# A spectral mixing and gated MLP kernel on one core: first item's copies, first loads, fewer warming matmuls, two loads on another queue

## The chip, the cores and the metric

The kernel runs on one core of one Trainium2 chip. The metric is the device time of one execution in microseconds (us). All times below are us unless marked ns. The profile comes from one profiled execution. Engines are called as the profile calls them: PE is TensorE (matmuls), PEld its weight loads, DVE is VectorE, ACT is ScalarE, POOL is GpSimd, SP is SyncE, which only issues DMAs here. A "q" behind an engine means its sequencer, which issues DMAs.

## What is computed

With x of 2048 x 512 (A_x; B_x isn't used), in float32:

```python
g = sigmoid((x * gate_w).sum(-1, keepdims=True))
a = dft_seq_re @ (x @ dft_hid_re.T) - dft_seq_im @ (x @ dft_hid_im.T)
b = (silu(x @ w1) * (x @ w3)) @ w2          # w1, w3: 512 x 1376, w2: 1376 x 512
out = g * a + (1 - g) * b
```

## The kernel before, in words

**Precision.** TensorE reads float32r operands. Every float32 operand is split in two: a high part, which is the source copied by ScalarE to float32r (`high`, L108), and a low part, which is source minus high part, subtracted by VectorE (`low`, L111). A product is then three matmuls, high x high, high x low, low x high (`mm3`, `matmul`, L122), accumulated in a PSUM bank of 128 x 512.

**Fast products.** Matrices are cut into 2 x 2 blocks and multiplied with seven block products instead of eight. This is why sums of blocks are formed on VectorE: `SUMS` for x (T1 to T4, L216), `sums_wb` for the weights (L255 to L258), `sum_c` (L698, L701) for the sequence matrices.

**First stage, the items.** An item is one chunk of 128 columns of w1 and w3 (the last chunk also holds the gate vector) with one half of the 2048 positions. `ITEMS` lists 9 chunks with half 0, then 2 chunks with both halves, then 9 with half 1. `gate_up(n)` does item n: groups of six matmuls, in order X (wb), Z (wb), the first product of item n+3 (X, wa), X (wb), Z (wa), the second product of item n+3 (Y, wa), X (wb). Between these, ScalarE and VectorE copy banks, form silu(gate) x up (L399, L414, in tile h), and split the weights of the items ahead. `store_h` sends the two halves of h to DRAM (hsp) from POOL's queue (L339). The lists `early`, `ahead`, `second`, `mid`, `at_end` hold further work for a given item. After each `prod(x, n, 3, 3)` VectorE adds the bank to u4 (L390), and `prod(x, n, 6, 2)` writes that bank again.

**Item 0** is written out by hand, with eight products instead of seven, since its operands arrive one after another. Loads all stand on SP's queue: the first weight block (128 KB, L233), the x block B11 (512 KB, L209), the other three weight blocks, then x blocks B21, B12, B22 and the weights of items 1 to 3. While they arrive, 11 matmuls of a constant run on TensorE (WARM, L425). Its four PSUM banks C00, C01, C10, C11 hold the two gate halves and the two up halves. Silu of C00 and C01 is made on ScalarE (tiles s1 and g1, L484, L500), and VectorE multiplies them with C10 and C11 straight from PSUM (L490, L508). `half(0, 0, 0, 0, ...)` is the first group; its order is high x high and low x high on the first half of B11, the same on the second half, then the two with B11's low part. `half(1, 0, None, 0, ...)` is the second group, on the fourth weight block (tile a). The next groups (wa, 12 matmuls) use B21.

**Second stage, the steps (P).** 12 matmuls a step for the first blocks, from about 207 on. Operands (zo) are split three steps ahead (`split_c(m + 3)`), summed four ahead, loaded eight ahead from SP's queue (B, L724). Functions in `todo` run ahead of a step's matmuls: `gates(0)` ahead of step 2 is ScalarE's sigmoid of the scores (tile p5g, L782), for which `load_score(0)` reads the scores from DRAM (gs), spread over all partitions; it stands right after the last item, on SP's queue (L772). `load_score(1)`, a block later, is on POOL's queue. Behind `gates(0)` in ScalarE's order stands `split_c(5)`. `late_load(i)` (L803) reads later weights, five or six steps ahead of their sums.

**Order.** The program order is kept as written on each engine and queue; an engine's instruction that waits holds up all behind it on that engine.

Of the kernel before, what the change touches and what calls it, by code (L numbers as in the profile page):

```python
# [7 lines left out]
F32 = mybir.dt.float32  # L8
F32R = mybir.dt.float32r
AF = mybir.ActivationFunctionType  # L10
ALU = mybir.AluOpType

P = 128
# [8 lines left out]
NG = NST // 2  # L22
NC = (F + P - 1) // P
NP2 = (NC + 1) // 2
WARM = 11
LOOK = 3
K = 9
W2_AT = (9, 11, 13, 15)
# [4 lines left out]
def fnet_swiglu_gate_kernel(  # L33
# [20 lines left out]
    nc = tc.nc  # L54

    def pool(name, bufs, side, space=None):
        kw = {} if space is None else {"space": space}
        cm = tc.tile_pool(name=name, bufs=bufs, side=side, reuse_waits="tile", **kw)
        return cm, cm.__enter__()
# [9 lines left out]
    xo0_cm, xo0 = pool("xo0", 1, "left")  # L69
    f4_a_cm, f4_a = pool("f4_a", 1, "right")  # L70
    wu_cm, wup = pool("wu", 1, "right")
    s1_cm, s1p = pool("s1", LOOK + 1, "right")
    wa_cm, wap = pool("wa", LOOK + 1, "right")
    wb_cm, wbp = pool("wb", 2, "right")
    u4_cm, u4p = pool("u4", 1, "right")
    h_cm, hp = pool("h", 2, "right")
    xo1_cm, xo1 = pool("xo1", 1, "right")
    gate_pools = (wu_cm, s1_cm, wa_cm, wb_cm, u4_cm, h_cm, xo1_cm)

    def bank(k, name):  # L80
        return psum.tile([P, 512], F32, tag=f"ps{k}", name=name)
# [14 lines left out]
    def wide(name):  # L96
        return take(F4, [P, 1024], F32, name)
# [9 lines left out]
    def high(hi, src):  # L107
        nc.scalar.activation(hi, src, AF.Copy)  # L108

    def low(hi, lo, src):  # L110
        nc.vector.tensor_sub(lo, src, hi.bitcast(F32))  # L111

    def split(hi, lo, src):
        high(hi, src)
        low(hi, lo, src)
# [5 lines left out]
    def matmul(ps, u, v, some=slice(None), **kw):  # L121
        nc.tensor.matmul(ps.rearrange("p (n a) -> p n a", a=2), u, turns(v)[:, some], **kw)  # L122

    def mm3(ps, ah, al, bh, bl, first, last, chain=False, some=slice(None)):
        for n, (u, v) in enumerate(((ah, bh), (ah, bl), (al, bh))):
            matmul(ps, u, v, some, start=first and n == 0, stop=last and n == 2,
                   skip_group_check=chain)
# [13 lines left out]
    def flat(ap):  # L141
        return ap.rearrange("p a n -> p (a n)")
# [33 lines left out]
    def forms2(r, t2, some):  # L176
# [4 lines left out]
        if 1 in some:  # L181
# [7 lines left out]
    ITEMS = ([(c, 0) for c in range(K)] + [(c, g) for c in range(K, NC) for g in range(2)]  # L189
             + [(c, 1) for c in range(K)])  # L190
    NI = len(ITEMS)
    SETS, WSET = [], []
# [5 lines left out]
    XO, ST = {}, {}  # L198
    XRAW = ("B12", "B11", "B21", "B22")

    def flat_x(ap):
        return ap.rearrange("p q n -> p (q n)")

    def load_xo(g, k):

        if g not in XO:
            XO[g] = (xo1 if g else xo0).tile([P, 2, 7, 2, 512], F32R, tag="xo", name=f"xo{g}")
        ST[g, k] = wide(f"xs{g}_{k}")
        nc.sync.dma_start(ST[g, k], xt[g, XRAW.index(k)])  # L209

    OPS = ("B11", "B21", "B22", "T1", "T2", "T3", "T4")
    SUMS = {"T1": ("B12", "B11"), "T2": ("B22", "T1"), "T3": ("B22", "B12"), "T4": ("B21", "T2")}

    def sum_xo(g, k, t):
        ST[g, k] = t
        nc.vector.tensor_sub(t, *(ST[g, v] for v in SUMS[k]))  # L216

    def xo_parts(g, k):
        o = XO[g][:, :, OPS.index(k)]
        return flat_x(o[:, 0]), flat_x(o[:, 1]), ST[g, k]  # L220

    def split_xo(g, k):
        split(*xo_parts(g, k))

    WS, WA, WB = {}, {}, {}
# [1 line left out]
    def back(w):  # L227
        return w >= NC and SETS[w] > 0

    def load_w(w, lo=0, hi=4):  # L230
        if lo == 0:
            WS[w] = f4_a.tile([P, 4, 256], F32, tag=f"f4_{4 + w % (LOOK + 1)}", name=f"ws{w}")
        nc.sync.dma_start(WS[w][:, lo:hi].rearrange("p a n -> p (a n)"),  # L233
                          w13[SETS[w], :, lo * 256 : hi * 256])

    def load_wb(w, spare=False):

# [4 lines left out]
    def wa_parts(w, lo, hi):  # L242
        return (*(flat(WA[w][:, h, lo:hi]) for h in range(2)), flat(WS[w][:, lo:hi]))

    def new_wa(w):

        WA[w] = wap.tile([P, 2, 3, 256], F32R, tag="wa", name=f"wa{w}")
# [27 lines left out]
    def prod(ps, n, wi, xi, start, chain=False):  # L275
        w = WSET[n]
        w, wi = (WA[w], wi) if wi < 3 else (WB[w], wi - 3)
        x = XO[ITEMS[n][1]]
        for q in range(2):
            sl = slice(q * P, (q + 1) * P)  # L280
            mm3(ps, w[:, 0, wi, sl], w[:, 1, wi, sl], x[:, 0, xi, q, :], x[:, 1, xi, q, :],
                start and q == 0, q == 1, chain)

    G = {}
# [4 lines left out]
    def prod1(n):  # L289
        x = bank(n % 4, f"X{n}")  # L290
        prod(x, n, 0, 0, True)
        return x
# [20 lines left out]
    def gate1(n):  # L313
        nc.scalar.activation(G[n][1], G[n][1], AF.Silu)
# [19 lines left out]
    def store_h(n, k, h):  # L334

        c, g = ITEMS[n]
        j = min(c % (NP2 - 1) if c < NC - 1 else NP2 - 1, NP2 - 1)
        b = 2 * (NP2 - 1 <= c < NC - 1)
        nc.gpsimd.dma_start(hsp[g, b + k, j // 2, :, j % 2 * 512 : (j % 2 + 1) * 512], h)  # L339
# [4 lines left out]
    early, ahead, second, mid, at_end = {}, {}, {}, {}, {}  # L344
# [72 lines left out]


    ctx.enter_context(tc.manual_schedule())
    load_w(0, 0, 1)  # L420
    load_xo(0, "B11")
    warm = nc.const_aps.tensor(1.0, [P, 512], mybir.dt.bfloat16)
    wps = bank(7, "wps")
    for n in range(WARM):
        nc.tensor.matmul(wps, warm[:, :P], warm, start=True, stop=True)  # L425
    nc.scalar.activation(act0, warm[:, :24], AF.Silu)
    load_w(0, 1, 4)
    for k in ("B21", "B12", "B22"):
        load_xo(0, k)
    load_w(1)  # L430
# [6 lines left out]
    C = {(i, j): bank((0, 4, 6, 7)[2 * i + j], f"C{i}{j}") for i in range(2) for j in range(2)}  # L437

    def half(i, j, w, x, start):

        wp = lambda h, sl: a21[:, h, sl] if w is None else WA[0][:, h, w, sl]
        xp = lambda q, h: b12[:, h, q * 512 : (q + 1) * 512] if x is None else XO[0][:, h, x, q, :]
        hh, lh, hl = (0, 0), (1, 0), (0, 1)
        order = [(r, *p) for r in range(2) for p in ((hh, hl, lh) if w is None else (hh, lh, hl))]
        if w == x == 0:
            order = [(r, *p) for some in ((hh, lh), (hl,)) for r in range(2) for p in some]
        for n, (r, u, v) in enumerate(order):
            matmul(C[i, j], wp(u, slice(r * P, (r + 1) * P)), xp(r, v),  # L450
                   start=start and n == 0, stop=not start and n == 5)

    def xo_half(k, q):
        i = OPS.index(k)
        return XO[0][:, 0, i, q], XO[0][:, 1, i, q], ST[0, k][:, q * 512 : (q + 1) * 512]

    s1 = s1p.tile([P, 512], F32, tag="s1", name="s1_0")
    g1 = u4p.tile([P, 512], F32, tag="u4", name="g1_0")
    h0 = hp.tile([P, 1024], F32, tag="h", name="h0")
    t1 = hp.tile([P, 1024], F32, tag="h", name="t1")  # L460
    new_wa(0)
    split(*wa_parts(0, 0, 1))

    def split_by_both(hi, lo, src):

        high(hi[:, :256], src[:, :256])
        nc.vector.tensor_copy(hi[:, 256:], src[:, 256:])
        low(hi, lo, src)

    split_by_both(*xo_half("B11", 0))  # L470
    split(*xo_half("B11", 1))
    half(0, 0, 0, 0, True)
    split(a21[:, 0], a21[:, 1], WS[0][:, 3])
# [7 lines left out]
    split(b12[:, 0], b12[:, 1], ST[0, "B12"])  # L481
    half(1, 0, 2, 1, False)
    split_xo(0, "B22")
    nc.scalar.activation(s1, C[0, 0], AF.Silu)  # L484
    half(0, 1, 0, None, True)
    WS.pop(0)
    load_w(4)
    sum_xo(0, "T1", t1)
    half(1, 1, None, None, True)
    nc.vector.tensor_mul(h0[:, :512], s1, C[1, 0])  # L490
    store_h(0, 0, h0[:, :512])
    sum_xo(0, "T2", ST[0, "B11"])
    half(0, 1, 1, 2, False)
    for w in (1, 2):
        new_wa(w)
        split(*wa_parts(w, 0, 3))
    half(1, 1, 2, 2, False)
    free(*zt)
    split_xo(0, "T2")
    nc.scalar.activation(g1, C[0, 1], AF.Silu)  # L500
    x1 = prod1(1)
    sums_wb(1)
    high(*xo_parts(0, "T1")[::2])
# [1 line left out]
    high(*wa_parts(3, 0, 3)[::2])  # L505
    y1 = prod2(1)
    copy_x(1, x1)
    nc.vector.tensor_mul(h0[:, 512:], g1, C[1, 1])  # L508
    store_h(0, 1, h0[:, 512:])
    x2 = prod1(2)  # L510
    high_wb(1)
    sum_g(1, y1)
# [2 lines left out]
    copy_x(2, x2)  # L515
    sum_xo(0, "T3", ST[0, "B12"])
    gate1(1)
    x3 = prod1(3)
    low_wb(1)
    high(*xo_parts(0, "T3")[::2])  # L520
# [7 lines left out]
    def do(work, n, f, *a):  # L528
        work.setdefault(n, []).append(lambda: f(*a))
# [9 lines left out]
    do(second, 1, free, *(ST[0, b] for b in ("B11", "B21", "B12", "B22")))  # L539
    do(second, 1, sum_g, 2, y2)  # L540
    do(mid, 1, gate1, 2)
    do(early, 2, sum_g, 3, y3)
    do(mid, 2, gate1, 3)

# [63 lines left out]
    for n in range(NI):  # L608
        if n in W2_AT:
            p = W2_AT.index(n)  # L610
# [4 lines left out]
        if n in A1_AT:  # L615
            p = A1_AT.index(n)
# [9 lines left out]
    n = NI - 1 - LOOK  # L626
# [142 lines left out]
    def load_score(g, queue):  # L769
        t, ng = GATES[g] = [flat(ut.tile([P, 2, 512], F32, tag=k, name=f"{k}g{g}"))  # L770
                            for k in ("p5", "u2")]
        queue.dma_start(t.rearrange("p (b n) -> p b n", b=2),  # L772
                        gs[2 * g : 2 * g + 2].rearrange("b o n -> o b n").to_broadcast([P, 2, 512]))
# [1 line left out]
    high_a(NG - 1)  # L775
    low_a(NG - 1)
    advance(-1)
    load_score(0, nc.sync)

    def gates(g):  # L780

# [18 lines left out]
    def late_load(i, src, tag):  # L800

        r, m = (flat(ut.tile([P, 2, 512], F32, tag=k, name=f"{k}p{i}")) for k in (tag, "c21"))
        nc.sync.dma_start(r, src)  # L803
        LATE[i] = [r, m]

    def late_pair(i, j):
# [207 lines left out]
    for i, (src, sp, p) in enumerate(late):  # L1014
        blk, b = 1 + i // 3, i % 3
        n = (10, 17, 24)[b]
# [89 lines left out]
```

## Time and profile before

| | |
|---|---|
| runs | 676.85, 676.11, 676.80 (median 676.8) |
| profiled execution | 676.03 |
| its span | 674.3 |
| VectorE busy | 601.5 (89%) |
| ScalarE busy | 370.4 (55%) |
| DMA, mean over the span | 256 GB/s |

The span is what the profile covers; the profiled execution's own time lies 1.7 above it. Busy shares are means over all stages. Matmuls are pipelined, so the duration of one (379 ns) is longer than the distance to the next. A timeline row reads: start, length, engine, line, operation, output <- inputs, shapes, count; in brackets the idle time of the engine ahead of it and what ended that. A windows row reads: stretch, its length, then busy time and count of PE, PEld, DVE, ACT, POOL, the granted clock, DMA share and GB/s. A chain row reads: start, length, what, count.

### The profile page before, as it was taken

Reading aid. Unit: us, or ns where it says so; the run is one execution under the profiler, and the core shown is the slowest. Engines: PE = TensorE matmul, PEld = TensorE weight load, DVE = VectorE, ACT = ScalarE, POOL = GpSimd, SP = SyncE. Lnnn points to the kernel's source line nnn. Section 1 sums busy time; section 2 is a strip of 40 time slices with the busy share of each in tenths; the row PEclk is TensorE's granted clock in tenths of the full one; section 3 lists DMA queues with packets and bytes.
Section 4 is the critical chain, followed back from the end, with each engine's and each line's share of the span. In section 5 each row is a group of like instructions: output and inputs, shape, how many; then the busy total and the mean of one; then the engine's idle time right before and its main releaser. Section 6 shows DMA issues by size and latency. Waiting matters only on the chain.

```text
span 674.3 us, 8670 instructions
## 1 busy us (share of the span) xinstructions
PE 670.3 (99%) x3101; PEld 583.8 (87%) x3101; DVE 601.5 (89%) x748; ACT 370.4 (55%) x494; POOL 64.5 (10%) x119
## 2 busy tenths in 40 slices
PE   9999999999999999999999999999999999999998
PEld 6888888888888888888888888888888888888887
DVE  6999988887679999988999899978896897898996
ACT  6676556655447764465554654554445455445451
POOL 0021112221110000001110101100000000000000
PEclk9999999999999999999999999999999999999999
DMA  7585547599998666815696279918986772873932
GB/s 296 209 306 220 228 192 265 189 337 381 414 418 301 251 215 225 294 63 207 220 387 246 89 246 354 366 57 351 391 330 249 281 256 89 312 279 154 342 130 93
DMA packets 45563, 172.54 MB, mean 256 GB/s; under 512 B 5328, under 2 KB 5712, under 8 KB 41680
## 3 DMA queue, kind: packets, MB, share of 16 engines
q1 hardware_dynamic: 32480, 118.11, 47.8%
q0 software_dynamic: 12752, 53.49, 20.2%
q8 instruction: 24, 0.39, 0.2%
q10 hardware_dynamic: 288, 0.39, 0.2%
q14 instruction: 19, 0.16, 0.1%
HBM read 114.82 MB, written 57.16 MB: 255 GB/s over the span
## 4 chain that ended last, share of the span: by engine, by line
PE 99%; DMA 0%; DVE 0%; ACT 0%; issue 0%
PE P L122 68%; PE X L122 16%; PE Z L122 8%; PE Y L122 4%; PE C L122 2%; PE wps L425 1%; DMA out<-zc 0%; DVE zc L856 0%; ACT zc L863 0%
## 5 line engine op out<-in xcount | busy, mean ns | idle before, releaser
L122 PE MATMUL P<-zo,a 128*128 128x512 f32 x1344 | 290.4, 379 | 0.0
L122 PEld LDWEIGHTS P<-zo,a 128*128 128x128 f32 x1344 | 253.8, 189 | 36.4 <-DVE zo L111 0.4
L108 ACT ACTIVATE zo<-B 128x1024 fp32r<-128x1024 f32 (+1 forms) x182 | 188.4, 1041 | 176.1 <-DVE B L698 74.1
L111 DVE TENSOR_TENSOR zo<-B,zo 128x1024 fp32r<-128x1024 f32 (+1 forms) x182 | 217.4, 1202 | 29.4 <-ACT zo L108 28.8
L122 PE MATMUL P<-zo,H 128*128 128x512 f32 x468 | 101.2, 379 | 0.0
L122 PEld LDWEIGHTS P<-zo,H 128*128 128x128 f32 x468 | 88.5, 189 | 12.6
L698 DVE TENSOR_TENSOR B<-B,B 128x1024 f32<-128x1024 f32 (+1 forms) x78 | 92.8, 1190 | 0.1
L122 PE MATMUL X<-xo,wb 128*128 128x512 f32 x378 | 88.6, 379 | 0.0
L122 PEld LDWEIGHTS X<-xo,wb 128*128 128x128 f32 x378 | 71.4, 189 | 10.2
L122 PE MATMUL P<-zo,Y 128*128 128x512 f32 (+1 forms) x336 | 71.6, 375 | 0.0
L122 PEld LDWEIGHTS P<-zo,Y 128*128 128x128 f32 x336 | 62.7, 189 | 8.7
L339 POOL DMA_DIRECT2D hsp<-h x42 | 23.0, 548 | 121.5 <-DVE h L399 70.4
L701 DVE TENSOR_TENSOR B<-B,B 128x1024 f32<-128x1024 f32 x26 | 31.7, 1219 | 0.0
L122 PE MATMUL X<-xo,wa 128*128 128x512 f32 x126 | 30.8, 380 | 0.0
L122 PE MATMUL Y<-xo,wa 128*128 128x512 f32 x126 | 30.6, 379 | 0.0
L122 PE MATMUL Z<-xo,wb 128*128 128x512 f32 x126 | 30.6, 379 | 0.0
L122 PE MATMUL Z<-xo,wa 128*128 128x512 f32 x126 | 30.6, 379 | 0.0
L122 PEld LDWEIGHTS X<-xo,wa 128*128 128x128 f32 x126 | 23.7, 189 | 3.6 <-DVE wa L111 0.3
L122 PEld LDWEIGHTS Y<-xo,wa 128*128 128x128 f32 x126 | 23.8, 189 | 3.4
L122 PEld LDWEIGHTS Z<-xo,wb 128*128 128x128 f32 x126 | 23.8, 189 | 3.4
L122 PEld LDWEIGHTS Z<-xo,wa 128*128 128x128 f32 x126 | 23.8, 189 | 3.4
L954 ACT ACTIVATE zu<-P 128x512 f32<-128x512 f32 x30 | 17.7, 596 | 15.2 <-PE P L122 12.7
(145 smaller groups left out, 551.4 us busy)
## 6 DMA issues: line engine op xcount, KB each, us to landing
B<-cc SPq DMA_DIRECT2D x64, 512.0 KB, 5.9
hsp<-h POOLq DMA_DIRECT2D x42, 256.0 KB, 3.9
B<-hsp SPq DMA_DIRECT2D x20, 512.0 KB, 5.6
wbsp<-wb POOLq DMA_DIRECT2D x8, 1024.0 KB, 4.2
wb<-wbsp SPq DMA_DIRECT2D x8, 1024.0 KB, 8.0
B<-zsp SPq DMA_DIRECT2D x16, 512.0 KB, 8.4
H<-w2sp SPq DMA_DIRECT2D x6, 1024.0 KB, 9.5
ws<-w SPq DMA_DIRECT2D x11, 512.0 KB, 4.3
```

The lines of the kernel that those rows point to most:

```text
L108: nc.scalar.activation(hi, src, AF.Copy)
L111: nc.vector.tensor_sub(lo, src, hi.bitcast(F32))
L122: nc.tensor.matmul(ps.rearrange("p (n a) -> p n a", a=2), u, turns(v)[:, some], **kw)
L339: nc.gpsimd.dma_start(hsp[g, b + k, j // 2, :, j % 2 * 512 : (j % 2 + 1) * 512], h)
L425: nc.tensor.matmul(wps, warm[:, :P], warm, start=True, stop=True)
L698: nc.vector.tensor_add(t, t, RAW[blk, b, q][:, :n])
L701: nc.vector.tensor_sub(t, RAW[blk, "B12", q], t)
L954: nc.scalar.activation(U[name][:, r], ps[r], AF.Copy)
```

## The change

Five things are done:

- `WARM` is 8 instead of 11.
- The first weight block and the fourth are loaded from ScalarE's queue, ahead of its first activation; the second and third from SP's queue. B11 is loaded in two DMAs of 512 columns. The high part of B11's first half is made by VectorE in one piece, ahead of the low part of the first weight block; before, ScalarE and VectorE made half of it each.
- Of item 0, C10 and C11 are copied from PSUM by ScalarE into a spare tile, beside the two silus. The two multiplications and their stores come later (`finish_first`), at the end of items 3 and 4, from SBUF.
- The spare tile lies where the seventh operand of the second x half will be, which gets a tile of its own (`xo_at`).
- `load_score(0)` and `late_load(0)` are issued from POOL's queue instead of SP's.

```diff
-WARM = 11
+WARM = 8
...
+    def xo_at(g, i):
+        if g == 0 or i < 6:
+            return XO[g][:, :, i]
+        if 2 not in XO:
+            XO[2] = xo1.tile([P, 2, 2, 512], F32R, tag="xo6", name="xo1_6")
+        return XO[2]
...
-        nc.sync.dma_start(ST[g, k], xt[g, XRAW.index(k)])
+        n = 512 if g == 0 and k == "B11" else 1024
+        for b in range(0, 1024, n):
+            nc.sync.dma_start(ST[g, k][:, b : b + n], xt[g, XRAW.index(k), :, b : b + n])
...
-    load_w(0, 0, 1)
+    load_w(0, 0, 1, nc.scalar)
     load_xo(0, "B11")
+    load_w(0, 3, 4, nc.scalar)
...
-    load_w(0, 1, 4)
+    load_w(0, 1, 3)
...
+    spare = xo1.tile([P, 2, 2, 512], F32, tag="xo6", name="spare")
+    first_h = [(spare[:, j, 0], spare[:, j, 1]) for j in range(2)]
+
+    def finish_first(j):
+        s, u = first_h[j]
+        nc.vector.tensor_mul(s, s, u)
+        store_h(0, j, s)
...
-    split(*wa_parts(0, 0, 1))
+    high(*wa_parts(0, 0, 1)[::2])
+    nc.vector.tensor_copy(*xo_half("B11", 0)[::2])
+    low(*wa_parts(0, 0, 1))
+    low(*xo_half("B11", 0))
...
-    split_by_both(*xo_half("B11", 0))
     split(*xo_half("B11", 1))
...
-    nc.scalar.activation(s1, C[0, 0], AF.Silu)
+    nc.scalar.activation(first_h[0][0], C[0, 0], AF.Silu)
...
-    nc.vector.tensor_mul(h0[:, :512], s1, C[1, 0])
-    store_h(0, 0, h0[:, :512])
...
+    nc.scalar.activation(first_h[0][1], C[1, 0], AF.Copy)
...
-    nc.scalar.activation(g1, C[0, 1], AF.Silu)
+    nc.scalar.activation(first_h[1][0], C[0, 1], AF.Silu)
...
-    nc.vector.tensor_mul(h0[:, 512:], g1, C[1, 1])
-    store_h(0, 1, h0[:, 512:])
...
     gate1(1)
+    nc.scalar.activation(first_h[1][1], C[1, 1], AF.Copy)
...
+    for j in range(2):
+        do(at_end, 3 + j, finish_first, j)
...
-    load_score(0, nc.sync)
+    load_score(0, nc.gpsimd)
...
-        nc.sync.dma_start(r, src)
+        (nc.sync if i else nc.gpsimd).dma_start(r, src)
```

More of the change, by code (lines that the diff above doesn't have):

```diff
@@ L202, in flat_x @@
         return ap.rearrange("p q n -> p (q n)")
+    def xo_at(g, i):
[4 more added lines that the diff above has]
+        return XO[2]
     def load_xo(g, k):
         if g not in XO:
-            XO[g] = (xo1 if g else xo0).tile([P, 2, 7, 2, 512], F32R, tag="xo", name=f"xo{g}")
+            XO[g] = (xo1 if g else xo0).tile([P, 2, 7 - g, 2, 512], F32R, tag="xo", name=f"xo{g}")
         ST[g, k] = wide(f"xs{g}_{k}")
-        nc.sync.dma_start(ST[g, k], xt[g, XRAW.index(k)])
+        n = 512 if g == 0 and k == "B11" else 1024
+        for b in range(0, 1024, n):
+            nc.sync.dma_start(ST[g, k][:, b : b + n], xt[g, XRAW.index(k), :, b : b + n])
     OPS = ("B11", "B21", "B22", "T1", "T2", "T3", "T4")
@@ L218, in xo_parts @@
     def xo_parts(g, k):
-        o = XO[g][:, :, OPS.index(k)]
+        o = xo_at(g, OPS.index(k))
         return flat_x(o[:, 0]), flat_x(o[:, 1]), ST[g, k]
@@ L228, in back, with load_w @@
         return w >= NC and SETS[w] > 0
-    def load_w(w, lo=0, hi=4):
+    def load_w(w, lo=0, hi=4, queue=nc.sync):
         if lo == 0:
             WS[w] = f4_a.tile([P, 4, 256], F32, tag=f"f4_{4 + w % (LOOK + 1)}", name=f"ws{w}")
-        nc.sync.dma_start(WS[w][:, lo:hi].rearrange("p a n -> p (a n)"),
-                          w13[SETS[w], :, lo * 256 : hi * 256])
+        queue.dma_start(WS[w][:, lo:hi].rearrange("p a n -> p (a n)"),
+                        w13[SETS[w], :, lo * 256 : hi * 256])
     def load_wb(w, spare=False):
@@ L277, in prod @@
         w, wi = (WA[w], wi) if wi < 3 else (WB[w], wi - 3)
-        x = XO[ITEMS[n][1]]
+        x = xo_at(ITEMS[n][1], xi)
         for q in range(2):
             sl = slice(q * P, (q + 1) * P)
-            mm3(ps, w[:, 0, wi, sl], w[:, 1, wi, sl], x[:, 0, xi, q, :], x[:, 1, xi, q, :],
+            mm3(ps, w[:, 0, wi, sl], w[:, 1, wi, sl], x[:, 0, q, :], x[:, 1, q, :],
                 start and q == 0, q == 1, chain)
@@ L455, in xo_half @@
         return XO[0][:, 0, i, q], XO[0][:, 1, i, q], ST[0, k][:, q * 512 : (q + 1) * 512]
-    s1 = s1p.tile([P, 512], F32, tag="s1", name="s1_0")
-    g1 = u4p.tile([P, 512], F32, tag="u4", name="g1_0")
-    h0 = hp.tile([P, 1024], F32, tag="h", name="h0")
+    spare = xo1.tile([P, 2, 2, 512], F32, tag="xo6", name="spare")
[4 more added lines that the diff above has]
+        store_h(0, j, s)
     t1 = hp.tile([P, 1024], F32, tag="h", name="t1")
     new_wa(0)
-    split(*wa_parts(0, 0, 1))
+    high(*wa_parts(0, 0, 1)[::2])
+    nc.vector.tensor_copy(*xo_half("B11", 0)[::2])
+    low(*wa_parts(0, 0, 1))
+    low(*xo_half("B11", 0))
     def split_by_both(hi, lo, src):
```

## The prediction

> **What bounds the kernel now.** I read the page first, then the chain of work that ended last, in order of time.
>
> ```profile
> PE 670.3 (99%) x3101; PEld 583.8 (87%) x3101; DVE 601.5 (89%) x748; ACT 370.4 (55%) x494; POOL 64.5 (10%) x119
> ```
>
> ```profile
> 0.78 4.85 PE wps L425 x11
> 5.63 11.03 PE C L122 x48
> ...
> 36.09 2.77 PE X L122 x12
> ...
> 41.44 2.59 PE X L122 x12
> ...
> 207.20 461.17 PE P L122 x2136
> ```
>
> TensorE is the chain from 0.78 to 668.4. Twelve matmuls of 512 columns take 2.59, so one takes 0.2158, and 2136 of them take 461.0 of the 461.17 shown. So nothing is to be gained after 207. Before it, two places exceed this rate: the 48 of C took 11.03 instead of 10.36, and the group at 36.09 took 0.18 too long. The 11 warming matmuls took 0.44 each, about twice 0.216: TensorE starts at half rate. The whole prize is therefore (part of) the warming time, 0.67 and 0.18. A loss has no such ceiling: with TensorE at 99%, whatever makes it wait is lost for good.
>
> The start, from the timeline and from the DMA view of the first 16 us (KB each, us from issue to landing):
>
> ```profile
> 0.73 1.28 ACT L426 ACT_TABLE_LOAD   x1 [0.73 <-PEq L1095]
> 1.17 0.42 SPq L209 DMA_DIRECT2D xs_B<-xt  x1
> 1.65 0.42 SPq L233 DMA_DIRECT2D ws<-w  x1
> 3.17 0.42 ACT L108 ACTIVATE wa<-ws 128x256 fp32r<-128x256 f32 x1 [0.92 <-DMA ws<-w]
> 4.98 0.29 DVE L467 CAST xo<-xs_B 128x256 fp32r<-128x256 f32 x1 [0.93 <-DMA xs_B<-xt]
> 5.43 1.29 DVE L111 TENSOR_TENSOR xo<-xs_B,xo 128x512 fp32r<-128x512 f32 x2 [0.15 <-ACT xo L108]
> 5.45 2.15 PE L122 MATMUL C<-xo,wa 128*128 128x512 f32 x6
> 7.43 1.46 PE L122 MATMUL C<-xo,a 128*128 128x512 f32 x6
> 7.88 1.30 DVE L111 TENSOR_TENSOR xo<-xs_B,xo 128x512 fp32r<-128x512 f32 x2 [0.15 <-ACT xo L108]
> 8.73 2.75 PE L122 MATMUL C<-xo,wa 128*128 128x512 f32 x12
> ```
>
> ```profile
> xs_B<-xt SPq DMA_DIRECT2D x4, 512.0 KB, 5.7
> ...
> ws<-w SPq DMA_DIRECT2D x1, 384.0 KB, 4.5
> ...
> ws<-w SPq DMA_DIRECT2D x1, 128.0 KB, 2.4
> ```
>
> B11 lands just before 4.98, 640 KB into the stream; the 384 KB behind it land at 1.65 + 4.5 = 6.15. So 256 KB take about 0.8 in a stream that is already full.
>
> **The change, part by part.**
>
> *The start.* Three warming matmuls go; at 0.44 each TensorE is free near 4.2 (8 x 0.44 after 0.78, its end overlapping the next). Its first real matmul now needs only the first 256 KB of B11: 4.97 less 0.8 gives 4.2, or up to 0.4 sooner, because that load is now first on SP's queue; I take 4.1. VectorE then casts 512 columns. The row for 256 says 0.29, and a 512-column subtraction takes 0.69: between these I take 0.43. First matmul near 4.6 instead of 5.45. The third one needs the second half of B11: 768 KB into the stream, 5.35 or up to 0.4 sooner, then a ScalarE copy of 512 columns (0.62, from the wa row's 0.42 for 256 plus 256 columns); I take 5.85. TensorE waits there for about 0.4. From there four at mixed rate end the group near 7.1, where it now ends at 7.43. **Gain 0.33**, bounds 0 and 0.59. It isn't below 0: even at 5.35 the second half is copied by 6.0, and the third matmul now comes 0.88 after 5.45, at 6.3. The upper bound is the next data: the third matmul of the x12 group at 8.73 reads, at 9.16, the low part ended at 7.88 + 0.69 = 8.57, whose load keeps its place in the saturated stream. Two DMA issues on ScalarE cost 0.42 each (SP's rows); they and the table load (1.28, from 0.73 now) end by 2.9, before the 3.17 at which ScalarE has data, so nothing.
>
> The trace shows that one issue on SP follows another after 0.42 plus a pause. The Trainium skill (Perfetto Trace Analysis, DMA Instruction — HWDGE) says that one descriptor generator serves both issuing engines and is locked for each DMA; then ScalarE's queue gives no head start and the gain would be about 0.2, by an estimate from the same rows. No row here shows two engines issuing at once.
>
> *Two multiplications off VectorE, two copies onto ScalarE.*
>
> ```profile
> 13.31 0.68 DVE L490 TENSOR_TENSOR h<-s,C 128x512 f32<-128x512 f32 x1
> 16.14 0.57 ACT L500 ACTIVATE g<-C 128x512 f32<-128x512 f32 x1
> 19.39 0.68 DVE L508 TENSOR_TENSOR h<-g,C 128x512 f32<-128x512 f32 x1
> 28.15 1.46 PE L122 MATMUL X<-xo,wb 128*128 128x512 f32 x6
> 30.04 0.68 DVE L390 TENSOR_TENSOR u<-u,X 128x512 f32<-128x512 f32 x1
> 35.42 0.95 DVE L111 TENSOR_TENSOR wa<-ws,wa 128x768 fp32r<-128x768 f32 x1
> 36.42 0.73 PEld L122 LDWEIGHTS X<-xo,wa 128*128 128x128 f32 x4 [0.31 <-DVE wa L111]
> ```
>
> ```profile
> 20.00:24.00 4.00, 4.00 (x20) 3.52 (x19) 4.00 (x7) 2.54 (x5) 0.55 (x1) 1.00 0.55 201
> ...
> 32.00:36.00 4.00, 4.00 (x20) 3.49 (x20) 3.94 (x7) 3.01 (x6) 1.08 (x2) 1.00 1.00 387
> ...
> 60.00:65.00 5.00, 5.00 (x25) 4.38 (x24) 4.97 (x7) 2.52 (x5) 1.09 (x2) 1.00 0.79 315
> ```
>
> In the windows (length, then PE, PEld, DVE, ACT, POOL) VectorE is busy all the time from 20 to 36, and the 0.18 at 36.4 is its queue arriving late. Without the two multiplications its queue runs up to 1.2 sooner, until L390, which must wait for TensorE's X (the group of 28.15 ends at 29.6): 0.3 of the lead survives, more than 0.18. **Gain 0.17** (bounds 0 and 0.18). The copies, 0.57 each, stand where ScalarE has gaps (busy 2.54 of 4 from 20 to 24): nothing.
>
> The multiplications come back at the end of items 3 and 4:
>
> ```profile
> 48.02 0.69 DVE L390 TENSOR_TENSOR u<-u,X 128x512 f32<-128x512 f32 x1 [1.18 <-PE X L122]
> 57.09 0.69 DVE L390 TENSOR_TENSOR u<-u,X 128x512 f32<-128x512 f32 x1
> 59.41 0.81 PE L122 MATMUL X<-xo,wb 128*128 128x512 f32 x3
> ```
>
> After 57 VectorE has hardly an idle moment (4.97 of 5 from 60 to 65), so two of about 0.6 put it 1.2 behind. TensorE's next writing of the same bank comes at 59.41, 1.63 after L390's end: 0.4 stays. Cost 0; if that cover is gone, up to 0.6 (one multiplication).
>
> *The score load to POOL's queue.* Here a wait is added.
>
> ```profile
> 207.04 14.20 PE L122 MATMUL P<-zo,a 128*128 128x512 f32 x65
> ```
>
> ```profile
> 207.23 0.33 SPq L772 DMA_DIRECT2D p5g<-gs  x1
> 208.27 1.23 POOL L339 DMA_DIRECT2D hsp<-h  x2 [5.25 <-DVE h L399]
> 214.19 1.04 ACT L782 ACTIVATE p5g<-p5g 128x1024 f32<-128x1024 f32 x1
> 215.49 1.07 ACT L108 ACTIVATE zo<-B 128x1024 fp32r<-128x1024 f32 x1 [0.27 <-DVE B L698]
> 217.56 1.22 DVE L111 TENSOR_TENSOR zo<-B,zo 128x1024 fp32r<-128x1024 f32 x1
> ```
>
> ```profile
> hsp<-h POOLq DMA_DIRECT2D x2, 256.0 KB, 7.9
> ```
>
> ```profile
> p5g<-gs POOLq DMA_DIRECT2D x1, 512.0 KB, 4.6
> ```
>
> Now SP issues it at 207.23 (it lands 5.4 later, and the sigmoid at 214.19 hardly waits). On POOL's queue it stands behind the last item's two hsp stores, so it is issued at 209.5 instead, and its bytes come behind theirs. These stores took 7.9 to land, to 216 and 217, since SP's loads (B, xs) fill the engines. Behind the sigmoid on ScalarE stands the high part of step 5's operand (the row at 215.49), behind that VectorE's low part (217.56). Step 5 of the P stage starts at 207.04 + 60 x 0.216 = 220.0 and needs the low part at its second matmul, 220.2. With L the landing: L + 1.0 (sigmoid) + 1.0 (high) + 1.3 (low) must be under 220.2, so L under 216.9. Every later microsecond is one of TensorE's. Bounds of L: 214.1 (209.5 + 4.6, the second score load, on POOL with SP's queue empty) and about 220 (217.2 as now, plus 2.8 for 512 KB). Without the score ahead of them, SP's loads finish sooner and the stores with them, by an amount no row shows; I take 218.0, nearest to the hsp rows. **Cost 1.1**, bounds 0 and 3.1. TensorE's wait is not made up, because it has no gap in the 448 us that follow.
>
> *late_load(0) to POOL:* its data are used five steps (13 us) after it, which is its cover; nothing. The smaller xo tile and its spare part change addresses only.
>
> *Sum*, from the profiled execution's 676.03 (span 674.3 and 1.7 around it): 676.03 - 0.33 - 0.17 + 1.1 = 676.6. The median of the runs shown is 676.8, 0.77 above it, so I add that: **677.4**.
>
> **The rivals.**
>
> *The score arrives in time* (under 216.9). For it: the second score load took 4.6 on POOL's queue, with a store of the same bytes just before it. Against: SP's queue was empty then and is full at 208. It gives 676.8 - 0.5 = 676.3.
>
> *The score arrives behind everything (slower).* The stores land at 217.2 as now, the score 2.8 or more later: TensorE stands 3 us in step 5. It decides from a landing of 218.8. For it: 7.9 of the hsp rows, with SP's loads ahead of them. Against: half of that jam was the score load itself, which leaves SP's queue. Time 676.8 - 0.5 + 2.9 = 679.2.
>
> *The clock.* The slow rate lasted from 0.78 to about 6.7 (the 0.67 lost in C is three matmuls' extra 0.22, from 5.45 on). If TensorE's pauses near 4.4 and 5.5 begin that time anew, half rate lasts to about 10.3 and costs 3.6/2 = 1.8. For it: warming has a purpose, and the pauses are new. Against: they are short, and no row shows one that slowed the rate. 676.8 - 0.2 + 1.8 + 1.1 = 679.5. The Trainium skill (TensorE: Matmul & The Clock Gate, Part 1) says that the full rate follows one busy window of about 3.4 us that runs free of the kernel; by an estimate from that page one missed window costs 1.7.
>
> *All of the warming is gained*: three warming matmuls' 1.28, 0.18, and no wait for the score: 675.3. Against it stands the 0.59 bound from B21's landing.
>
> **How the numbers follow.** About 0.2% (1.35 us) is what a measurement of this kernel can tell from no change. Chances: forecast (some wait for the score, 0.3 to 1.9 us) 0.45; score in time 0.28; score behind everything 0.20; clock 0.04; all of the warming 0.03. Only the last is faster by over 0.2%: 0.03. Slower by more: 0.20 + 0.04, and 0.03 of the forecast's upper end: 0.27. Within: 0.70. The range goes from the in-time case less 0.4 for a deeper gain at the start (675.9) to the late case (679.2).
>
> **What would show it.** Right: first C matmul near 4.6, a pause of some 0.4 before the third, the group on a at about 7.1; no wait for wa near 36; the sigmoid waiting for the DMA of p5g, and TensorE waiting for VectorE's zo about 13 us into P. Wrong: p5g landing less than 9.8 after the first P matmul, L390 ending after TensorE wants the bank (57 to 70), or C matmuls 0.44 apart beyond 7.

## The result and the profile after

The changed kernel takes **683.07** (median of 6 runs, 680.90 to 685.33) against 676.36 for the kernel before (6 runs, 676.11 to 676.85). The ratio is 1.010, 95% interval 1.009 to 1.011: slower by 6.7. The forecast was 677.4, 0.6 above the 676.8 that it set out from, with a range of 675.9 to 679.2; the time lies outside that range.

The profiled execution took 685.33, its span is 683.5. First the page:

```profile
PE 673.8 (99%) x3098; PEld 586.2 (86%) x3098; DVE 602.1 (88%) x748; ACT 371.3 (54%) x495; POOL 65.6 (10%) x121
PE   8999999999999799999999999999999999999998
PEclk9999999999999899999999999999999999999999
```

The shares of busy time are as before: nothing in them says that 9 us are lost. The slices do. Between the two ends, one slice dips in the row of TensorE and in the row of its clock: the fourteenth, which is 222 to 239. That is the P stage, some steps in. The chain of waits (start, length, what) says why:

```profile
211.21 12.02 DMA p5g<-gs
223.23 0.02 issue
223.25 0.04 ACT p5g L800
223.29 0.92 issue
224.21 1.05 ACT zo L108
225.26 0.02 issue
225.28 1.24 DVE zo L111
226.52 0.04 issue
226.56 450.99 PE P L122 x2075
```

Before, the chain ran through TensorE alone. Now it begins with the score load: issued at 211.21, landed at 223.23, then the sigmoid (L800, the old L782), the high and the low part of step 5's operand, and only then TensorE. The waits of TensorE up to 240 (total, times, longest) give the size:

```profile
PE P L122 <- ACT zo L108: 3.5, 1, 3.5
PE C L122 <- ACT wa L108: 1.6, 1, 1.6
...
PE P L122 <- DVE zo L111: 0.5, 1, 0.5
```

There is a second new wait, 1.6 in C at the start. From the timeline of the start:

```profile
0.73 0.89 ACTq L243 DMA_DIRECT2D ws<-w  x2
0.74 0.85 SPq L219 DMA_DIRECT2D xs_B<-xt  x2
0.78 3.18 PE L436 MATMUL wps<-const-bfloat16-1.0 128*128 128x512 bf16 x8 [0.78 <-PEq L1113]
4.88 0.43 DVE L479 CAST xo<-xs_B 128x512 fp32r<-128x512 f32 x1 [4.88 <-DMA xs_B<-xt]
5.06 0.42 ACT L108 ACTIVATE wa<-ws 128x256 fp32r<-128x256 f32 x1 [1.88 <-DMA ws<-w]
5.53 2.91 PE L122 MATMUL C<-xo,wa 128*128 128x512 f32 x6 [1.57 <-ACT wa L108]
...
8.23 2.46 PE L122 MATMUL C<-xo,a 128*128 128x512 f32 x6
```

The weights, first on a queue of their own, are there at 5.04; before they were there at 3.15. The first half of B11 is there at 4.86, hardly sooner than the whole of it was. So the first real matmul starts at 5.53 (5.45 before, 4.6 forecast), and then something else shows: the group on a takes 2.46 where it took 1.46. The windows (stretch, length, busy time and count of PE, PEld, DVE, ACT, POOL, granted clock, DMA share, GB/s), cut at the places where the granted clock changes, show the rate:

```profile
0.00:3.43 3.43, 2.65 (x7) 1.01 (x8) 0.00 (x0) 1.51 (x2) 0.19 (x4) 1.00 0.43 80
3.43:6.84 3.41, 1.73 (x6) 0.64 (x5) 1.73 (x4) 1.36 (x4) 0.00 (x0) 1.00 0.99 370
6.84:10.26 3.42, 3.42 (x9) 2.71 (x9) 2.99 (x7) 2.52 (x4) 0.00 (x0) 0.50 1.03 420
10.26:13.60 3.34, 3.34 (x17) 2.90 (x17) 3.27 (x3) 2.63 (x4) 0.00 (x0) 1.00 1.02 413
...
221.88:225.30 3.42, 0.00 (x0) 0.00 (x0) 0.02 (x1) 2.05 (x3) 0.00 (x0) 1.00 0.66 271
225.30:228.70 3.40, 2.93 (x6) 2.07 (x7) 3.40 (x4) 3.40 (x6) 0.00 (x0) 0.50 0.02 10
228.70:232.10 3.40, 3.40 (x9) 2.68 (x9) 3.40 (x4) 2.08 (x3) 1.07 (x2) 0.50 0.26 105
232.10:235.50 3.40, 3.40 (x17) 2.97 (x17) 3.40 (x4) 2.01 (x2) 0.00 (x0) 1.00 0.89 294
```

Read the counts beside the clock: a full stretch of 3.4 holds 17 matmuls at full rate and 9 at half, so one stretch at half rate costs about 8 x 0.216 = 1.7. (The clock column shows 1.00 until its first record, also over the warming matmuls, which run at half rate; at the start only the counts tell.) TensorE had reached full rate at 3.43, paused for 1.57, was busy for only 1.73 of the stretch, and ran the next one at half rate. After the stop at 221.9 it ran two stretches at half rate.

That accounts for the profiled execution. P begins at 208.67 instead of 207.04: 1.63 lost at the start. The matmul that needs the low part of step 5 has 61 ahead of it and would start at 208.67 + 61 x 0.216 = 221.84; it starts at 226.56: **4.72** is the stop. From there 2075 matmuls take 450.99 instead of 448.2: 2.8 are half rate. The sum is 9.15; P ends at 677.55 instead of 668.37, which is 9.18. The other runs lie below 685.33; the mean granted clock over their spans is 0.994 in one and 0.997 in four, against 0.992 here. One stretch at half rate lowers the mean by 0.0025, so four of them have one such stretch and one has two, where this one has three.

### The profile page after: what moved, and what is told of

Its sections match the earlier page's. It is cut to its first block, busy times and chain, and to the rows that moved or that the text cites. A ratio compares the mean times of both kernels' runs of the same rounds, so it can differ in the third digit from the quotient of the medians.

```text
span 683.5 us, 8668 instructions
## 1 busy us (share of the span) xinstructions
PE 673.8 (99%) x3098; PEld 586.2 (86%) x3098; DVE 602.1 (88%) x748; ACT 371.3 (54%) x495; POOL 65.6 (10%) x121
## 4 chain that ended last, share of the span: by engine, by line
PE 66%; DMA 2%; DVE 0%; ACT 0%; issue 0%
PE P L122 66%; DMA p5g<-gs 2%; DMA out<-zc 0%; DVE zo L111 0%; ACT zo L108 0%; DVE zc L874 0%; ACT zc L881 0%; ACT p5g L800 0%
## 5 line engine op out<-in xcount | busy, mean ns | idle before, releaser
L122 PE MATMUL P<-zo,a 128*128 128x512 f32 x1344 | 294.0, 382 | 4.0 <-ACT zo L108 3.5
```

## The experiments

All times are medians; each group was run beside its own runs of the kernel before on the same chip (676.25 of 24 runs, 676.31 of 31, 676.26 of 27). Names: "after" and "before" are the two kernels of the change.

**1. Only the score load, undone and alone.** In after, back to SP's queue; in before, to POOL's queue.

```diff
# in after:
-    load_score(0, nc.gpsimd)
+    load_score(0, nc.sync)
# in before:
-    load_score(0, nc.sync)
+    load_score(0, nc.gpsimd)
```

> The changed kernel with the first score load back on SP's queue. Theory (place on the queue): the score lands within 6 us of its issue, TensorE does not stop in P, no half-rate stretch follows there; what stays is the slower start (first X group at 18.3 instead of 16.5, with one half-rate stretch from 6.8 to 10.3), so about 677.5, 1.1 over the kernel before. Rival (the start's delay or the other DMAs cause the stop in P): the stop near 220 stays at about 4 us and the time stays over 681.

> The kernel before with nothing changed but the first score load on POOL's queue. Theory: it lands some 12 us after its issue, behind the two hsp stores; TensorE stops for 4 to 5 us at step 5 of P and then runs at half rate for one or more stretches of 3.4 us (1.7 us each): 681 to 684.5. Rival (the stop needs the other parts of the change, which let SP's loads go out sooner): under 679.

Measured: undone, 677.89 (ratio to before 1.002, interval 1.001 to 1.003), which is 5.2 less than after. Alone in before, 682.06 (4 runs; ratio 1.0076, 1.0057 to 1.0095), which is 5.8 more than before by the medians, and 5.1 by the ratio (interval 3.9 to 6.4). The one line makes most of the loss. The expectations missed in detail: the trace of the undone kernel has no half-rate stretch at the start (its first X group is at 16.97, not 18.3), and in before the load landed 10.8 after its issue and the stop was 3.54, a little under what was expected. From the timeline of before with the load on POOL's queue:

```profile
221.75 1.06 ACT L782 ACTIVATE p5g<-p5g 128x1024 f32<-128x1024 f32 x1 [6.16 <-DMA p5g<-gs]
...
223.81 0.48 PE L122 MATMUL P<-zo,a 128*128 128x512 f32 x1 [2.34 <-ACT zo L108]
225.07 6.30 PE L122 MATMUL P<-zo,a 128*128 128x512 f32 x21 [0.78 <-DVE zo L111]
```

Its windows around the stop:

```profile
221.32:224.73 3.41, 0.64 (x2) 0.19 (x1) 0.94 (x1) 2.98 (x4) 0.00 (x0) 1.00 0.72 294
224.73:228.14 3.41, 3.07 (x7) 2.52 (x8) 3.41 (x4) 3.41 (x6) 0.00 (x0) 0.50 0.01 5
228.14:231.50 3.36, 3.36 (x17) 2.92 (x16) 3.36 (x4) 1.95 (x3) 1.06 (x2) 1.00 0.48 190
```

ScalarE waits 6.16 for the scores, TensorE 2.34 and 0.78 for what stands behind them, and then comes one stretch at half rate, which 7 matmuls touch. One run, 680.36, had a mean clock of 1.0: there the stop alone cost about 680.36 - 676.25 = 4.1. The other three (681.57 to 682.77) had 0.997, the mean that one such stretch gives.

**2. The place of the sigmoid.** Before with the score load on POOL's queue, but the functions that use the scores of block 0 two steps later, behind the operands of steps 5 and 6 in ScalarE's order.

```diff
-        at(g, 2 + g, gates, g)
+        at(g, 4 - g, gates, g)
...
-            at(g, 3 + g + j, gate_row, g, j)
-        at(g, 5 + g, store_gates, g)
+            at(g, 5 - g + j, gate_row, g, j)
+        at(g, 7 - g, store_gates, g)
```

> The kernel before with the first score load on POOL's queue, and the work on the scores (sigmoid, the two rows, the stores) two steps later, which is 5.2 us. Theory (the whole loss is ScalarE's queue held up by the sigmoid, and the half rate that follows): the score still lands about 11 us after its issue, but the sigmoid comes by then; TensorE does not stop, no half rate, 676.3. Rival (the score's late load slows the sequence loads B or the stores, and TensorE stops for these): a stop in P of over 1 us stays, over 678.

Measured: 676.45, ratio 1.0005 (0.9996 to 1.0015): the loss is gone. The load is as slow as in experiment 1, by the DMA view of 205 to 212:

```profile
p5g<-gs POOLq DMA_DIRECT2D x1, 512.0 KB, 10.7
```

From its timeline, the sigmoid and TensorE:

```profile
220.44 1.06 ACT L782 ACTIVATE p5g<-p5g 128x1024 f32<-128x1024 f32 x1 [0.50 <-DMA p5g<-gs]
...
208.69 17.66 PE L122 MATMUL P<-zo,a 128*128 128x512 f32 x81
```

81 matmuls run in a row across the place of the stop. So neither the late load nor traffic around it stops TensorE, but the place at which ScalarE waits for it.

**3. Another second queue.** Before with the score load on ScalarE's queue, where no store stands ahead of it.

```diff
-    load_score(0, nc.sync)
+    load_score(0, nc.scalar)
```

> The kernel before with the first score load on ScalarE's queue. It is issued behind ScalarE's splits, near 209.7, so 2.5 later than on SP's queue and as late as on POOL's, but with no stores ahead of it. Theory (place behind the two stores and POOL's late entry into the engines make the 11 us): it lands 5 to 8 us after its issue, by 217.5, TensorE stops for under 1 us, 676.3 to 677.5. Rival (any queue is late once SP's loads are out): it lands 10 us or more after its issue, and the stop is over 3 us, 680 or more.

Measured: 676.25, ratio 1.0001 (0.9992 to 1.0011), and no stop in the trace. The load was issued at 207.53, sooner than I had expected, and landed 9.5 later, at 217.06. From its DMA view of 205 to 212 (queues: packets, MB, share; then the issues), and from its timeline:

```profile
q1 hardware_dynamic: 420, 1.54, 63.8%
q0 software_dynamic: 41, 0.12, 4.4%
q10 hardware_dynamic: 7, 0.03, 1.3%
...
p5g<-gs ACTq DMA_DIRECT2D x1, 512.0 KB, 9.5
```

```profile
217.08 1.06 ACT L782 ACTIVATE p5g<-p5g 128x1024 f32<-128x1024 f32 x1 [2.61 <-DMA p5g<-gs]
```

q10 carries this one load: its first packet moved 4.1 us after the issue, and by 212 it had moved 7, while SP's queue (q1) moved 1.54 MB in these 7 us. On SP's queue the same load takes 5.5 (experiment 1, undone). So it is late on a queue without any store ahead, too. The time and the landing were those of the theory; the delay of 9.5 lies between the two expectations. The margin was 0.02 (the limit is worked out below), and one of the ten runs, at 678.82 with a mean clock of 0.997, fits a landing beyond it; it was not traced. On POOL's queue the load is issued 2.5 after the first P matmul instead of 0.3, behind two stores, and takes 10.7 to 12.0. How much of that added delay is the stores and how much POOL's queue itself, no run separates.

**4. The start: warming alone, and the rest with 11.** Before with 8 warming matmuls; after with the score load on SP's queue and 11.

```diff
# in before:
-WARM = 11
+WARM = 8
# in after with the score load on SP's queue:
-WARM = 8
+WARM = 11
```

> The kernel before with 8 warming matmuls, all else as it was. First real matmul at 5.45 as before, so TensorE pauses from 4.35 for 1.1 us. Theory (a pause within a window drops or delays the full rate): in executions where the pause falls into the window that decides, half rate lasts 3.4 us longer, 1.7 us: median 676.5 to 678. Rival (the length of the warming is nothing as long as the data come at 5.4): 676.3.

> The changed kernel with the score on SP's queue and 11 warming matmuls. Theory (the pause of 1.6 us, not the loads, costs most of the start): TensorE is busy to 5.0, the pause is 0.6, no half-rate stretch from 6.8 on; the later landing of B21 (7.9 instead of 7.4) bounds the start, first X group at 16.8 to 17.0, 676.6. Rival (the loads' lateness is the cost, the clock is not): first X group still after 17.8, 677.5.

Measured: 8 alone costs 0.9 (677.19; ratio 1.0012, 1.0003 to 1.0021). Back at 11, the rest of the change takes 676.29 (ratio 0.9999, 0.9990 to 1.0009), 1.6 less than the 677.89 with 8; TensorE had no pause there, where 0.6 was expected. Windows of before with 8:

```profile
2.71:6.13 3.42, 2.21 (x5) 0.80 (x4) 1.31 (x3) 1.43 (x4) 0.00 (x0) 1.00 0.96 365
6.13:9.54 3.41, 3.41 (x9) 2.69 (x8) 3.21 (x8) 2.73 (x5) 0.00 (x0) 1.00 1.03 418
9.54:13.00 3.46, 3.46 (x17) 3.02 (x16) 3.27 (x3) 2.48 (x5) 0.00 (x0) 1.00 1.02 416
```

With 8, TensorE has a pause of 1.21 before its first real matmul, at 5.56; the stretch around the pause is 2.21 busy, and the next still holds 9 matmuls. Full rate comes at 9.54. In before, with no such pause, it came at 6.67, behind this stretch:

```profile
3.26:6.67 3.41, 3.41 (x9) 1.63 (x8) 1.96 (x5) 1.82 (x5) 0.00 (x0) 1.00 1.02 401
```

The moment moves by itself from one execution to the next: it was 4.10, 4.35, 6.24 and 6.28 in the four other traced kernels that start like before. So the 0.9 is a median over such executions, and this one trace shows how the time is lost, not how often.

**5. The start: which load is late.** First, after with the score load on SP's queue and both early weight blocks on SP's queue too, behind each other with the halves of B11. Then, in before with 11: the whole of the loads' part; only the weight blocks on ScalarE's queue; only B11 in two loads.

```diff
# weights on ScalarE's queue (alone, or with the halves and VectorE's cast):
-    load_w(0, 0, 1)
+    load_w(0, 0, 1, nc.scalar)
     load_xo(0, "B11")
+    load_w(0, 3, 4, nc.scalar)
...
-    load_w(0, 1, 4)
+    load_w(0, 1, 3)
# B11 in two loads (alone, or with the weights):
-        nc.sync.dma_start(ST[g, k], xt[g, XRAW.index(k)])
+        n = 512 if g == 0 and k == "B11" else 1024
+        for b in range(0, 1024, n):
+            nc.sync.dma_start(ST[g, k][:, b : b + n], xt[g, XRAW.index(k), :, b : b + n])
```

> The changed kernel with the score on SP's queue and the weight blocks of item 0 on SP's queue too, the first ahead of B11 as before; B11 still in two loads, 8 warming matmuls. Theory (ScalarE's queue made the first weights late): they land near 3.2 instead of 5.0, the first half of B11 near 4.5, first matmul near 5.0, TensorE idle for about 1.0 instead of 1.6; first X group at 16.3 to 16.8 if the full rate holds, 676.2. Rival (the idle time alone, not its cause, sets off the half rate): still a half-rate stretch from about 6.8, first X group at 17.5 or later, 677.5.

> The kernel before with only the loads' part of the change: B11 in two loads, its first half's high part by VectorE, the first and fourth weight block on ScalarE's queue; 11 warming matmuls. Theory (the new order of loads loses): the first weights land at 4.4 to 5.0 instead of 3.15 and B21 0.3 to 0.5 later, so the part costs 0.3 to 0.8: 676.9. Rival (with the warming long enough the loads are harmless): 676.3.

> The kernel before with only the first and fourth weight block on ScalarE's queue, B11 whole. Theory (two queues at once share the slow first microseconds): the first weights land after 4.2 though nothing is ahead of them on their queue, B11 near 5.0 as before; high and low of the weights then come after B11's, 676.5 to 677. Rival (the halving made them late): they land near 3.2, 676.3.

> The kernel before with only B11 in two loads, all on SP's queue, weights first. Theory (a load of half the bytes in rows of half the length lands hardly sooner at the start): the first half lands at 4.6 to 5.4, not at 4.2, and gains nothing: 676.3 to 676.8. Rival (the prediction's reckoning of 0.8 us for 256 KB): the first half lands near 4.2, first matmul near 4.8, 676.0.

| kernel | median | ratio to before (95%) | first weights there | first B11 data there | first C matmul |
|---|---|---|---|---|---|
| after, score and weights on SP | 678.22 | 1.0029 (1.0019 to 1.0039) | 3.10 | 5.43 (half) | 6.03 |
| before + loads' part | 676.95 | 1.0011 (1.0002 to 1.0020) | 4.33 | 4.17 (half) | 4.82 |
| before + weights on ScalarE's queue | 677.11 | 1.0017 (1.0007 to 1.0026) | 5.05 | 4.88 (whole) | 6.30 |
| before + B11 in halves | 678.08 | 1.0027 (1.0015 to 1.0040) | 3.15 | 4.82 (half) | 5.31 |

None gains. The first one missed its theory: the weights are early, as theorised, but the halves of B11 behind them came late. Its rival was right in the late first X group (17.71), but not in the cause: TensorE idles for 1.68, and still no half-rate stretch follows, as the group on a shows:

```profile
6.03 1.97 PE L122 MATMUL C<-xo,wa 128*128 128x512 f32 x6 [1.68 <-DVE xo L479]
...
7.83 1.46 PE L122 MATMUL C<-xo,a 128*128 128x512 f32 x6
```

B11 in halves alone cost 1.8, where 0.5 at most was expected. The two parts of the loads do not add up, either: 0.9 and 1.8 alone, 0.7 together. Of the two parts alone, the second queue makes the weights late even with B11 whole; from that kernel's timeline:

```profile
5.07 0.42 ACT L108 ACTIVATE wa<-ws 128x256 fp32r<-128x256 f32 x1 [1.89 <-DMA ws<-w]
...
6.30 1.79 PE L122 MATMUL C<-xo,wa 128*128 128x512 f32 x6 [1.02 <-DVE xo L468]
```

And the halving brings the first half hardly sooner than the whole (4.82, against 4.92 to 5.24 in the seven traces with weights first and B11 whole), while B21, the next x block, lands at 8.45 instead of 7.41; from the timeline with B11 in halves, where ScalarE and then TensorE wait for B21:

```profile
8.47 0.94 ACT L108 ACTIVATE xo<-xs_B 128x256 fp32r<-128x256 f32 x2 [0.99 <-DMA xs_B<-xt]
...
8.94 2.29 PE L122 MATMUL C<-xo,wa 128*128 128x512 f32 x8 [0.25 <-ACT xo L108]
```

The late x blocks cost more on VectorE than here. The chain that ended last in this kernel runs from the last x block's landing at 11.00 mostly through VectorE, and TensorE takes over near 37, about 0.9 later than in experiment 2's trace (36.56):

```profile
3.54 7.46 DMA xs_B<-xt
...
37.49 2.43 PE X L122 x10
```

**6. The first item's copies alone.** Before with only the copies of C10 and C11, the spare tile and the two later multiplications; then the same with one warming matmul less.

```diff
# in before:
-    nc.vector.tensor_mul(h0[:, :512], s1, C[1, 0])
-    store_h(0, 0, h0[:, :512])
...
+    nc.scalar.activation(first_h[0][1], C[1, 0], AF.Copy)
...
+    for j in range(2):
+        do(at_end, 3 + j, finish_first, j)
# then:
-WARM = 11
+WARM = 10
```

> The kernel before with only item 0's part of the change: C10 and C11 copied by ScalarE, the multiplications at the end of items 3 and 4, the spare tile. Theory: the wait for wa near 36 (0.18) goes and nothing comes for it, 676.1. Rival (VectorE's queue, 1.2 behind after item 4, is late for the bank that L390 reads): a TensorE wait of 0.3 to 0.6 between 59 and 80, 676.6.

> Item 0's part alone (the version that was fastest) with 10 warming matmuls. Theory (a short pause costs nothing, only one near a third of the deciding stretch does): the pause grows by 0.43, 675.6 as with 11. Rival (every pause ahead of the first product makes the full rate come later in some executions): 675.9 to 676.4.

Measured: **675.59**, ratio 0.9990 (0.9981 to 0.9999), 0.7 below before and the fastest version in this study; with 10 warming matmuls 676.07, ratio 0.9994 (0.9984 to 1.0003), no gain over 11 and within the rival's 675.9 to 676.4. The group near 36, of the timeline with the copies alone, has no wait in it:

```profile
35.87 1.46 PE L122 MATMUL X<-xo,wa 128*128 128x512 f32 x6
```

## Why the prediction was wrong, step by step

The parts measured alone add up: score load +5.8, loads +0.7, warming +0.9, first item -0.7 make +6.7, which is what the whole change costs, though the intervals leave room (3.9 to 6.4 for the score load). Taken off the changed kernel one after another they do so too: 5.2 for the score load, 1.6 for the warming, and 0.0 for what is left.

**The score load to POOL's queue** is the step that failed most: cost 1.1 forecast, 5.8 measured. Its mechanism was right in every link (the sigmoid waits, the operand of step 5 behind it, the low part, TensorE), and so was its limit. The limit is 9.86 after the first P matmul; a landing later than that should stop TensorE for the difference:

| kernel | score lands after the first P matmul | less 9.86 | stop measured |
|---|---|---|---|
| before, score on ScalarE's queue | 9.84 | 0 | none |
| before, score on POOL's queue | 13.38 | 3.52 | 3.54 |
| after | 14.56 | 4.70 | 4.72 |

(The landing is the end of the DMA in the chain or the start of the waiting sigmoid less 0.02; the stop is the start of the first matmul behind it, less the first P matmul's start and 61 x 0.216. The limit itself is 216.9 less 207.04.) What was mis-sized is the landing L: taken as 10.96 after the first P matmul (218.0), bounded at about 13 (220), and it was 13.4 to 14.6. The reason that I gave for a value below the bound, that SP's loads get done sooner without the score among them, was no row; the nearest rows, those of the hsp stores on the same queue, said 216 to 217 and then 512 KB more. The rival "behind everything" has this mechanism, and its 2.9 was too small as well.

The same step left out what a stop does to the rate. Behind it TensorE ran one or two stretches of 3.4 at half rate, at 1.7 each. The rival **the clock** named this mechanism with its price (1.7 to 1.8), but put it at the start only and gave it 0.04. In the profiled execution it came at both places; by the mean clocks above, four of the other five runs had one such stretch in all. The argument against it, that "no row shows one that slowed the rate", was empty: before has no pause of TensorE at full rate longer than the 0.18 near 36, so no row could have shown it. The Trainium skill (TensorE: Matmul & The Clock Gate, "HAM oscillation — how this bites in real kernels") gives the rule that gaps of over some 3.4 us are what re-throttles. The trace differs: a wait of 2.34, in a stretch of 3.41 that was busy for 0.64, did it in experiment 1, and a pause of 1.57 in the start of after. A pause of 1.68 (experiment 5, first kernel), of which 1.21 fell into a stretch at full rate, did not.

**The start**: gain 0.33 forecast, and "It isn't below 0"; measured a loss of 0.7 for the loads and 0.9 for the warming (1.6 where the loads were in). Two terms fell. The first is the loads. The first half of B11 was to land at 4.1, with the weights there as before at 3.15. The weights came at 5.04, and at 4.50, 4.43 and 4.33 in the three other traces with the same loads (experiments 1, 4 and 5): ScalarE's queue made them 1.2 to 1.9 late. The first half came at 4.86, and at 4.33, 4.26 and 4.17 in those three, so its size was about right when the weights had left SP's queue; it was the weights that the first matmul waited for. The second term is the warming. Three warming matmuls fewer were counted as time given back; what they did, in the traces of before with 11 and with 8, was to keep TensorE busy up to its first data, so that full rate came a stretch sooner. The reason given for the bound at 0 looked at the data of B11 alone, not at the weights and not at the rate. What the 1.6 consists of in the usual run of after with the score load on SP's queue is not shown: its traced run (676.84) is faster than the median (677.89), and a full rate that comes late doesn't show in the mean clock.

**Two multiplications off VectorE**: right in kind, wait near 36 gone; 0.17 forecast, 0.7 measured (interval 0.1 to 1.3, which holds the forecast). The profile of before happened to show a small wait there, 0.18. The wait stands in six of the eight traces without the copies (0.31 to 0.72 idle in the row of the weight load) and in none of the six with them. It was larger in the other five than in before, as in this row of before with the sigmoid later, where full rate had come sooner and TensorE reached the place ahead of VectorE's queue:

```profile
36.56 0.73 PEld L122 LDWEIGHTS X<-xo,wa 128*128 128x128 f32 x4 [0.71 <-DVE wa L111]
```

In before 0.31 of idle cost 0.18; 0.71 would cost some 0.6, by an estimate from the two rows. That this accounts for all of the 0.7 is argued, not shown. The wait also means that in before a sooner start soon meets VectorE's queue near 36, a limit that the prediction's "whole prize" left out.

**The multiplications come back** at the end of items 3 and 4: cost 0, right. From the timeline of after:

```profile
59.19 0.68 DVE L400 TENSOR_TENSOR u<-u,X 128x512 f32<-128x512 f32 x1
...
61.04 2.32 PE L122 MATMUL X<-xo,wb 128*128 128x512 f32 x10
```

L400 is the old L390: it ends at 59.87, and TensorE writes the bank again from 61.04 on, with no gap ahead of it. **late_load(0)** at nothing: with it and the first item, the loads' part and 11 warming matmuls the time is 676.29, so no cost is seen.

Of the signs that were listed, the sigmoid's wait for p5g, TensorE's wait for zo 13 us into P and the missing wait near 36 came; the first C near 4.6 and the group on a near 7.1 did not, and "C matmuls 0.44 apart beyond 7", listed as a sign against, did.

**Open**: what exactly decides the rate. At full rate a stretch 1.73 busy of 3.41 was followed by half rate, and stretches of 2.17 and 2.36 (after with the score load on SP's queue, with and without the weights there) were not. At half rate 2.65 busy led to full rate and 2.21 did not, but 2.93 after the stop of after didn't either, and 3.07 after that of experiment 1 did. One bound on the busy column doesn't order all of these. But that column holds each matmul's whole duration, 0.63 at half rate, where the distance from start to start is 0.43. Summed by that distance (0.216 at full rate), these stretches and some more of the same traces do fall in order: at half rate 1.87, 2.42 and 2.48 were followed by half rate and 2.65, 2.70, 2.74 and 2.92 by full rate; at full rate 0, 0.2 and 1.0 were followed by half rate and 1.67 and 1.70 were not. So matmul work per stretch fits these traces, but no run was made to test it. Why a second queue's bytes come so late was not settled either, only that they do.

## What to carry to other kernels

A load moved off a loaded queue isn't free of that queue: take its landing from rows of the target queue at that moment, and look on the waiting engine for what stands behind the waiting instruction. If the load can't be made earlier, move its consumer back by as many steps as it is late; that took the whole loss away here. Where TensorE is the bound, price a new stop at its length plus a stretch of half rate (here none to two), and count warming matmuls by the data that they bridge to, not by their own time.

## What the runs showed of the hardware

- Two loads of 256 KB on one queue, behind the weights, landed at 4.82 and 5.47 where one of 512 KB landed at 4.92 to 5.24, and in that trace the block behind them came 1.0 later than in before. I had expected half the data in half the remaining time. With the weights on ScalarE's queue the first half came at 4.17 to 4.86.
- 128 KB issued at 0.73 took 3.6 to 4.3 to land on ScalarE's queue beside SP's loads (2.4 on SP's queue, as the first load there). The Trainium skill (DMA: Bandwidth & Descriptors, "Latency and other measured facts") has a first byte after about 0.6 on either of these queues. The trace differs at a busy moment: the first packet on ScalarE's queue (q10) came 4.1 after its issue in experiment 3, and 1.6 after it at the start of after.
- The issues themselves did not wait for one another: two on ScalarE's sequencer took 0.89 and two on SP's 0.85, both from 0.73 on. The late part lies behind the issue.
- A pause of 1.57 at full rate, in a stretch 51% busy, was followed by 3.4 us at half rate; one of 1.68, of which 1.21 fell into a stretch at full rate that was 64% busy, was not.
